# Gated linear attention and two MoE layers: the prefix levels of all four batches taken together, steps laid out by place in their group of four

## The chip, the core and the metric

The kernel runs on one core of one Trainium2 chip. The metric is the device time of one execution in microseconds. The engines named below are PE (matrix products), DVE (vector), ACT (scalar functions and copies), POOL (a second, general engine) and SP (here only an issuer of DMAs).

## What is computed

Four batches of eight heads, 768 steps, 48 dimensions. Attention keeps a complex state of 48 x 48 per head, of which only the real part is fed and read:

```python
mag = sqrt(a_re**2 + a_im**2)
scale = minimum(mag, 0.999) / (mag + 1e-06)
a_re_n, a_im_n = a_re * scale, a_im * scale
for t in range(768):
    S_re, S_im = ar * S_re - ai * S_im + outer(k[t], v[t]), ar * S_im + ai * S_re
    y[t] = q[t] @ S_re
x = tokens(y)                                # 3072 x 384
h = x @ w1_in                                # 384 -> 2048
x = (maximum(h, 0) + alpha * minimum(h, 0)) @ w1_out
h = x @ w2_in
out = where(h >= 1, h, where(h <= -1, 0, (h + 1)**2 / 4)) @ w2_out
```

The weights come as float64 words.

## The kernel before

**Attention.** The steps are cut into six chunks of 128. A *pair* is two batches of one chunk; there are twelve, first batches 0 and 1 for all chunks, then batches 2 and 3. A *slab* is one batch of a pair; `qkh0_1` is that of slab 1 of pair 0. On chip a pair's decays lie in tile `C`, 128 partitions x (re, im) x 6 rows x 129 columns, where column 0 is the carry. For each pair:
- `front` (L155 to L171) normalises the decays; ACT and DVE alternate.
- `scans` (L179 to L185) runs one bounded scan over 768 elements (L182) with the bound `cap`, whose first column takes the carry `mie` of the pair before.
- `levels` takes prefix products of the complex decays with `cmul` (L140 to L147): `ta` within groups of 4 neighbouring steps, `tb` over 4 groups, `tc` and `td` over those, `te` back over the groups. A `cmul` is two multiplications, or four if the shape has more dimensions (L144), into a scratch tile, then one subtraction and one addition back into `C`. With steps in their natural order the operands of `ta` are 16 bytes apart. At its end POOL (L214 to L220) makes the next pair's carry.
- `half`, once for each slab: a last `cmul` (`tf`), two products `qkh` (L231), and 12 DMAs (L235, L238) that restack `qkh` into tile `st`.
- `slab_matmul`: scores `sp` on PE from `st`, `am` = masked scores on DVE (L254), `yp` on PE, then `xbuf` (high part by ACT, L278, low part by DVE, L279), and the update of `state`.

**MoE.** Layer 1 takes blocks of 1, 1, 2, 2, 2, 2 and 2 pairs (256 or 512 columns), layer 2 six blocks of 512. Every product is three matrix products of high and low parts. For each of 16 slices `fc` of the hidden width a block does `h` on PE (9 matmuls, L360), the evacuation, and `acc` on PE (9 matmuls, L392). In layer 1 the evacuation is ACT `u` (L372) and `t` (L373), DVE `t` (L374), ACT `gh` (L380), DVE `gl` (L381).

**Weights.** `load_raw` loads 393 KB of words for each half of a slice; `decode` makes float32 of them in one ACT and four DVE instructions (L306 to L312), 384 elements wide; PE and ACT make the high and low parts (L341 to L346). The loads of slices 7 to 15 are put behind the restacking DMAs of slab 0 of pair 0 in SP's queue.

**Order.** A scheduler sets one static order for each engine when the kernel is built; the instructions of an engine then run in that order, each when its semaphores allow. Evacuations have priority. The source interleaves the steps of attention, of the next pair's `front` and `scans`, and of the decoding:

```python
def attention(p):
    if p + 1 < NPAIR:
        load_pair(p + 1)
    yield from levels(p)
    ahead = prepare(p + 1) if p + 1 < NPAIR else iter(())
    yield from interleave(slabs(p), ahead, SIDE)
    yield from ahead
```

## Time and profile before

| | us |
|---|---|
| median of 3 runs | 1110.85 (1109.9 to 1111.08) |
| profiled execution: span | 1106.8 |
| PE busy | 1008.4 (91%) |
| DVE busy | 853.1 (77%) |
| ACT busy | 515.3 (47%) |
| POOL busy | 96.7 (9%) |

The profiled execution is one of its own; its span runs from the first to the last instruction, and the runs' median is 4.05 us above it, which is what lies around a span. Busy shares are means over the whole program: the first half has attention and layer 1, the second hardly more than matrix products.

### The profile page before, as it was taken

The numbers are of one execution on the slowest core, as the hardware profiler recorded it, in microseconds if no ns is written. First come the engines' busy times: TensorE is split into PE (matmuls) and PEld (weight loads), VectorE is DVE, ScalarE is ACT, GpSimd is POOL, SyncE is SP. The second block draws the span as 40 slices with busy tenths as digits, with TensorE's granted clock in tenths as the row PEclk, the third lists the DMA queues.
The fourth block names the chain that finished last, engine by engine and source line by source line (L and its number), as shares of the span: only waits on it lengthen the run. The fifth ranks groups of instructions, "written<-read, shape, count | busy, mean of one in ns | idle before, by whom it ended". The sixth has DMA issues, their size and how long they took to land.

```text
span 1106.8 us, 16614 instructions
## 1 busy us (share of the span) xinstructions
PE 1008.4 (91%) x6113; PEld 820.4 (74%) x6113; DVE 853.1 (77%) x1858; ACT 515.3 (47%) x920; POOL 96.7 (9%) x116
## 2 busy tenths in 40 slices
...
GB/s 305 80 291 21 113 24 84 97 105 46 102 118 60 114 118 35 147 59 76 122 71 69 51 158 191 144 1 58 1 1 57 1 58 1 1 29 1 29 1 31
DMA packets 59929, 84.93 MB, mean 77 GB/s; under 512 B 7488, under 2 KB 35904, under 8 KB 59840
## 3 DMA queue, kind: packets, MB, share of 16 engines
...
q14 instruction: 39, 0.32, 0.1%
...
## 4 chain that ended last, share of the span: by engine, by line
PE 50%; DVE 31%; DMA 7%; issue 3%; POOL 3%; ACT 2%; SPq 2%; DVEq 0%; ACTq 0%; POOLq 0%
PE acc L392 24%; PE h L360 23%; DVE qkh L231 3%; DVE gl L381 2%; DMA C<-in_ri 2%; DVE C L146 2%; DMA rawhi<-in_w 2%; DVE C L147 2%; DVE t L374 2%; DVE tf L144 2%; DVE ab L182 2%; POOL cw L214 1%; DVE am L254 1%; DMA st<-qkh 1%; DVE C L171 1%
## 5 line engine op out<-in xcount | busy, mean ns | idle before, releaser
L360 PE MATMUL h<-xbuf,whi 128*128 128x512 f32 (+1 forms) x1212 | 374.9, 385 | 4.6 <-ACT wlo L346 3.2
L360 PEld LDWEIGHTS h<-xbuf,whi 128*128 128x128 f32 x1212 | 223.3, 191 | 52.9 <-ACT wlo L346 4.4
L392 PE MATMUL acc<-gl,whi 128*128 128x512 f32 (+1 forms) x606 | 230.1, 383 | 3.7 <-DVE gl L381 3.4
L380 ACT ACTIVATE gh<-t 128x512 fp32r<-128x512 f32 (+1 forms) x208 | 124.4, 598 | 232.3 <-DVE t L374 114.7
L360 PE MATMUL h<-xbuf,wlo 128*128 128x512 f32 (+1 forms) x606 | 231.4, 382 | 0.0
L392 PE MATMUL acc<-gh,wlo 128*128 128x512 f32 (+1 forms) x606 | 228.1, 381 | 0.0
L392 PE MATMUL acc<-gh,whi 128*128 128x512 f32 (+1 forms) x606 | 206.4, 384 | 3.9 <-ACT gh L380 3.3
L381 DVE TENSOR_TENSOR gl<-t,gh 128x512 fp32r<-128x512 f32 (+1 forms) x208 | 134.7, 649 | 67.1 <-ACT gh L380 65.8
L378 DVE TENSOR_TENSOR m<-h,t 128x512 f32<-128x512 f32 x96 | 66.3, 692 | 111.8 <-ACT t L376 111.8
L392 PEld LDWEIGHTS acc<-gl,whi 128*128 128x128 f32 x606 | 114.7, 189 | 29.7 <-DVE gl L381 7.2
L360 PEld LDWEIGHTS h<-xbuf,wlo 128*128 128x128 f32 x606 | 115.7, 191 | 22.3 <-issue 0.2
L392 PEld LDWEIGHTS acc<-gh,wlo 128*128 128x128 f32 x606 | 114.6, 189 | 22.5 <-issue 0.4
L392 PEld LDWEIGHTS acc<-gh,whi 128*128 128x128 f32 x606 | 110.6, 189 | 27.5 <-ACT gh L380 5.2
L376 ACT ACTIVATE t<-h 128x512 f32<-128x512 f32 x96 | 57.5, 599 | 124.5 <-PE h L360 113.6
L372 ACT ACTIVATE u<-h,sg 128x512 f32<-128x512 f32 (+1 forms) x112 | 69.2, 618 | 54.8 <-PE h L360 54.6
L374 DVE TENSOR_TENSOR t<-u,t 128x512 f32<-128x512 f32 (+1 forms) x112 | 68.7, 613 | 27.9 <-ACT t L373 27.9
L252 PE MATMUL sp<-st 96*128 96x128 f32 x384 | 64.2, 300 | 21.4 <-DMA st<-qkh 19.0
L252 PEld LDWEIGHTS sp<-st 96*128 96x128 f32 x384 | 59.7, 212 | 32.1 <-issue 22.6
L344 PE MATMUL wd<-wfirst,ident 128*128 128x384 f32 x64 | 35.4, 649 | 44.3 <-DVE wfirst L312 22.9
L373 ACT ACTIVATE t<-h,sal 128x512 f32<-128x512 f32 (+1 forms) x112 | 69.4, 620 | 6.5 <-DMA x2d<-o 6.5
L379 DVE SCALAR_TENSOR_TENSOR t<-t,m 128x512 f32<-128x512 f32 x96 | 66.1, 691 | 2.6
L214 POOL TENSOR_TENSOR cw<-C 128x12 f32<-128x12 f32 (+1 forms) x13 | 25.6, 1971 | 311.7 <-DVE C L147 311.7
...
## 6 DMA issues: line engine op xcount, KB each, us to landing
...
rawhi<-in_w SPq DMA_DIRECT2D x31, 384.0 KB, 4.5
rawlo<-in_w SPq DMA_DIRECT2D x31, 384.0 KB, 5.0
...
C<-in_ri SPq DMA_DIRECT2D x22, 384.0 KB, 5.8
...
```

The lines of the kernel that those rows point to most:

```text
L214: G.tensor_tensor(w[:, 0:2], co, co, op=ALU.mult)
L252: nc.tensor.matmul(sp[:, h], st[0:96, slot(4 * f + h, 1)], st[0:96, slot(4 * f + h, 0)], start=True, stop=True)
L360: nc.tensor.matmul(hp[:, :n], wt[:, ws], xt[:, kk, :n], start=(k == 0), stop=(k == 8))
L372: A.activation(u[:, :n], hp[:, :n], AF.Copy, scale=sg[:, fc:fc + 1])
L373: A.activation(t[:, :n], hp[:, :n], AF.Copy, scale=sal[:, fc:fc + 1])
L374: V.tensor_tensor(t[:, :n], u[:, :n], t[:, :n], op=ALU.max)
L376: A.activation(t[:, :n], hp[:, :n], AF.Relu, scale=0.5, bias=0.5)
L378: V.tensor_tensor(m[:, :n], hp[:, :n], t[:, :n], op=ALU.max)
L379: V.scalar_tensor_tensor(t[:, :n], t[:, :n], 1.0, m[:, :n], op0=ALU.min, op1=ALU.mult)
L380: A.activation(gh[:, :n], t[:, :n], AF.Copy)
L381: V.tensor_tensor(gl[:, :n], t[:, :n], gh[:, :n].bitcast(F32), op=ALU.subtract)
L392: nc.tensor.matmul(blk["acc"][m][:, :n], wt[:, ws], gt[:, :n], start=(fc == 0 and q == 0), stop=(fc == NFC - 1 and q == 2))
```

## The change

- Pairs go chunk by chunk: pairs 0 and 1 are batches 0 and 1, then 2 and 3, of chunk 0. `levels` takes all twelve rows of a chunk at once (chunk 0 in parts of 3, 3 and 6 rows), so six sets of levels do the work of twelve.
- The 128 steps of a chunk are laid out by their place in the group of four: four runs of 32 columns. `ta` and `tf` then work on runs of 32 neighbours; `tb` steps by 16 bytes. The host lays out inputs and outputs to suit; the mask follows.
- `cmul` writes one product in place and needs half the scratch. Instruction counts of a `cmul` stay.
- The scan runs over the products of groups (33 columns for each row in place of 128), with three small multiplications ahead of it and one (576 elements) behind; `k` is multiplied in `scans`. POOL writes the carry into `cap` itself, and the DVE instruction that did (L179) is gone.
- `C` is twice as large, in two buffers; `q` and `k` have tiles and loads of their own. The second half of chunk 0 is loaded by two DMAs of its own.
- Evacuation of layer 1: one ACT pass and tile `u` go; DVE takes `max(h*sal, t)` straight from PSUM with a scalar for each partition; `gh` and `gl` are multiplied by `sg` in place of the weights, whose own ACT pass (L340 before) goes.
- `decode` is 768 wide: one set of instructions for each slice in place of two.
- The scratch for dynamic DMAs is set to 512.

```diff
     def cmul(name, b, a, dims):
-        sh = [128, 2, *dims]
+        t = t[:, :, 0:w].rearrange(f"p n ({dn}) -> p n {dn}", **{f"d{i}": d for i, d in enumerate(dims)})
         if sum(d > 1 for d in dims) < 3:
-            V.tensor_tensor(t1, a(0).to_broadcast(sh), b, op=ALU.mult)
-            V.tensor_tensor(t2, a(1).to_broadcast(sh), b, op=ALU.mult)
+            sh = [128, 2, *dims]
+            V.tensor_tensor(t, a(1).to_broadcast(sh), b, op=ALU.mult)
+            V.tensor_tensor(b, a(0).to_broadcast(sh), b, op=ALU.mult)
         else:
-            for k in range(4):
-                V.tensor_tensor((t1, t2)[k // 2][:, k % 2], a(k // 2).to_broadcast([128, 1, *dims])[:, 0], b[:, k % 2], op=ALU.mult)
-        yield
-        V.tensor_tensor(b[:, 0], t1[:, 0], t2[:, 1], op=ALU.subtract)
-        V.tensor_tensor(b[:, 1], t1[:, 1], t2[:, 0], op=ALU.add)
-        yield
...
+    def scans(c, js):
+        nj = js.stop - js.start
+        h, o = divmod(js.start, NJ)
+        m = tmps.pop((c, js.start))[:, 2, 0:nj].rearrange("p j (a g) -> p j a g", a=GI)
+        V.tensor_tensor(m[:, :, 2], m[:, :, 2], m[:, :, 3], op=ALU.mult)
+        V.tensor_tensor(m[:, :, 1], m[:, :, 1], m[:, :, 2], op=ALU.mult)
+        f = fac[:, o:o + nj]
+        V.tensor_tensor(f[:, :, 1:], m[:, :, 0], m[:, :, 1], op=ALU.mult)
+        yield
+        s = p1.tile([128, NJ, NG + 1], F32, tag="S", name=f"S{c}_{js.start}")[:, 0:nj]
+        flat = [x.rearrange("p j g -> p (j g)") for x in (s, f, cap[:, js])]
         V.tensor_tensor_scan(flat[0], flat[1], flat[2], 1.0, op0=ALU.mult, op1=ALU.min)
         yield
-        G.tensor_copy(mis[p][:, js], a[:, :, T - 1])
-        A.activation(m2, a, AF.Square)
-        yield
+        V.tensor_tensor(m[:, :, 1:], m[:, :, 1:], s[:, :, 0:NG].unsqueeze(2).to_broadcast([128, nj, GI - 1, NG]), op=ALU.mult)
+        G.tensor_copy(mis[c][:, js], s[:, :, NG])
+        A.activation(m[:, :, 0], s[:, :, 1:], AF.Square)
+        A.activation(m[:, :, 1:], m[:, :, 1:], AF.Square)
+        yield
+        k = ks[2 * c + h][:, o:o + nj]
+        V.tensor_tensor(k, k, m.rearrange("p j a g -> p j (a g)"), op=ALU.mult)
+        yield
...
-        # prefix products: within groups of 4, of 4 groups, of 8 of those with the carry
-        g = C[:, :, :, 1:].rearrange("p n j (g i) -> p n j g i", i=4)
-        for i in range(1, 4):
-            yield from cmul(f"ta{p}_{js.start}__{i}", g[:, :, :, :, i], lambda n: g[:, n:n + 1, :, :, i - 1], (nj, T // 4))
-        e = C[:, :, :, 1:].rearrange("p n j (u w) -> p n j u w", w=16)
-        V.tensor_tensor(q2[:, 1], q2[:, 1], m2, op=ALU.mult)
-        for w in (7, 11, 15):
-            yield from cmul(f"tb{p}_{js.start}__{w}", e[:, :, :, :, w], lambda n: e[:, n:n + 1, :, :, w - 4], (nj, NU))
-        yield from cmul(f"tc{p}_{js.start}_", C[:, :, :, 16], lambda n: C[:, n:n + 1, :, 0], (nj,))
+            A.activation(C[:, :, :, 0], Cs[c - 1][:, :, js, NG], AF.Copy)
+        def place(i):
+            return C[:, :, :, 1 + NG * (GI - 1 - i):1 + NG * (GI - i)]
+        nm = f"{c}_{js.start}"
+        for i in range(1, GI):
+            yield from cmul(f"ta{nm}__{i}", place(i), lambda n: place(i - 1)[:, n:n + 1], (nj, NG))
+        e = place(GI - 1).rearrange("p n j (u v) -> p n j u v", v=4)
+        for w in range(1, 4):
+            yield from cmul(f"tb{nm}__{w}", e[:, :, :, :, w], lambda n: e[:, n:n + 1, :, :, w - 1], (nj, NU))
+        yield from cmul(f"tc{nm}_", C[:, :, :, 4], lambda n: C[:, n:n + 1, :, 0], (nj,))
         for k in (1, 2, 4):
-            z = e[:, :, :, :, 15].rearrange("p n j (y z) -> p n j y z", z=2 * k)
-            yield from cmul(f"td{p}_{js.start}__{k}", z[:, :, :, :, k:], lambda n: z[:, n:n + 1, :, :, k - 1:k], (nj, 4 // k, k))
-        h = C[:, :, :, 0:T].rearrange("p n j (u w) -> p n j u w", w=16)
-        yield from cmul(f"te{p}_{js.start}_", e[:, :, :, :, 3:15:4], lambda n: h[:, n:n + 1, :, :, 0:1], (nj, NU, 3))
-        # |P|^2 MI^2 of the chunk's end: near one, and what is off goes into the carry
-        co = C[:, :, :, T]
-        w = p1.tile([128, 3, nj], F32, tag="cw", name=f"cw{p}_{js.start}")
+            z = e[:, :, :, :, 3].rearrange("p n j (y z) -> p n j y z", z=2 * k)
+            yield from cmul(f"td{nm}__{k}", z[:, :, :, :, k:], lambda n: z[:, n:n + 1, :, :, k - 1:k], (nj, 4 // k, k))
+        h = C[:, :, :, 0:NG].rearrange("p n j (u v) -> p n j u v", v=4)
+        yield from cmul(f"te{nm}_", e[:, :, :, :, 0:3], lambda n: h[:, n:n + 1, :, :, 0:1], (nj, NU, 3))
...
+        w = p1.tile([128, 3, NR], F32, tag="cw", name=f"cw{nm}")[:, :, 0:nj]
         G.tensor_tensor(w[:, 0:2], co, co, op=ALU.mult)
         G.tensor_tensor(w[:, 0], w[:, 0], w[:, 1], op=ALU.add)
         G.tensor_tensor(w[:, 1], mie, mie, op=ALU.mult)
-        G.tensor_tensor(chk[:, p, 0, js], w[:, 0], w[:, 1], op=ALU.mult)
-        G.tensor_copy(chk[:, p, 1, js], mie)
-        G.tensor_scalar(w[:, 2], chk[:, p, 0, js], -0.5, 1.5, op0=ALU.mult, op1=ALU.add)
-        G.tensor_tensor(mie, mie, w[:, 2], op=ALU.mult)
+        G.tensor_tensor(chk[:, c, 0, js], w[:, 0], w[:, 1], op=ALU.mult)
+        G.tensor_copy(chk[:, c, 1, js], mie)
+        if c < NC - 1:
+            G.tensor_scalar(w[:, 2], chk[:, c, 0, js], -0.5, 1.5, op0=ALU.mult, op1=ALU.add)
+            G.tensor_tensor(cap[:, js, 0], mie, w[:, 2], op=ALU.mult)
+    def fixup(c, js):
+        nj = js.stop - js.start
+        C = Cs[c][:, :, js]
+        dst = C[:, :, :, 1 + NG:].rearrange("p n j (a g) -> p n j a g", g=NG)
+        yield from cmul(f"tf{c}_{js.start}", dst, lambda n: C[:, n:n + 1, :, 0:NG].unsqueeze(3), (nj, GI - 1, NG))
...
-            if layer == 1 and s == 1:
-                A.activation(w, w, AF.Copy, scale=sg[:, fc:fc + 1])
...
         if layer == 1:
-            u = p2.tile([128, 512], F32, tag="u", name=f"u{nm}", bufs=UB)
-            A.activation(u[:, :n], hp[:, :n], AF.Copy, scale=sg[:, fc:fc + 1])
-            A.activation(t[:, :n], hp[:, :n], AF.Copy, scale=sal[:, fc:fc + 1])
-            V.tensor_tensor(t[:, :n], u[:, :n], t[:, :n], op=ALU.max)
+            A.activation(t, hp, AF.Copy, scale=sg[:, fc:fc + 1])
+            V.scalar_tensor_tensor(t, hp, sal[:, fc:fc + 1], t, op0=ALU.mult, op1=ALU.max)
+            A.activation(gh, t, AF.Copy, scale=sg[:, fc:fc + 1])
+            V.scalar_tensor_tensor(gl, t, sg[:, fc:fc + 1], gh.bitcast(F32), op0=ALU.mult, op1=ALU.subtract)
...
+    def attention(c):
+        if c + 1 < NC:
+            load_chunk(c + 1)
+            load_k(2 * c + 2)
+        yield from levels(c, ALL)
+        def ahead():
+            yield from prepare(c + 1, HALVES[0])
+            load_k(2 * c + 3)
+            yield from prepare(c + 1, HALVES[1])
+        ahead = ahead() if c + 1 < NC else iter(())
+        yield from interleave(chain(slabs(2 * c), slabs(2 * c + 1)), ahead, SIDE)
         yield from ahead
...
+    load_rows(0, HALVES[1])
+    load_k(1)
+    run(interleave(prepare(0, HALVES[1]), weights, E1))
+    run(interleave(attention_second(), weights, E2))
...
-        while blk["layer"] == 1 and attn < min(NPAIR, blk["p0"] + 4):
+        while blk["layer"] == 1 and attn < min(NC, blk["p0"] // 2 + 2):
```

DVE's order behind the second slab's `qkh` in the kernel before: the products, the next pair's `ta`, its scan and decoding (`wfirst`) follow, and `am0_1_0` stands twenty rows behind them.

```order
L231 TENSOR_TENSOR qkh0_1_524<-C0_109,qk0_117 128x2x384 x2
L140 TENSOR_TENSOR ta1_0__1_852<-C1_613 128x2x192
L141 TENSOR_TENSOR ta1_0__1_852<-C1_613 128x2x192
L311 SCALAR_TENSOR_TENSOR wfirst_95<-rawlo1_3_132,wfirst_95 128x384
L182 SCALAR_TENSOR_TENSOR ab1_616<-m21_617,cap_98 128x768
L307 TENSOR_SCALAR wfirst_95<-wfirst_95 128x384
L146 TENSOR_TENSOR C1_613<-ta1_0__1_852 128x6x32
L147 TENSOR_TENSOR C1_613<-ta1_0__1_852 128x6x32
L312 SCALAR_TENSOR_TENSOR wfirst_95<-rawlo1_3_132,wfirst_95 128x384
L310 TENSOR_SCALAR wfirst_95<-wfirst_95 128x384
L140 TENSOR_TENSOR ta1_0__2_898<-C1_613 128x2x192
L141 TENSOR_TENSOR ta1_0__2_898<-C1_613 128x2x192
```

The same place in the changed kernel: `ab0_6` is the `front` of rows 6 to 11 of chunk 0, whose input is a square that ACT takes of the second half of `C0`.

```order
L263 TENSOR_TENSOR qkh0_1_511<-C0_115,q0_127 128x2x384
L263 TENSOR_TENSOR qkh0_1_511<-C0_115,k0_120 128x2x384
L172 SCALAR_TENSOR_TENSOR ab0_6_594<-ab0_6_594 128x768
L286 TENSOR_TENSOR am0_1_0_533<-sp0_1_0_528,mask_86 128x512
L177 SCALAR_TENSOR_TENSOR ab0_6_594<-ab0_6_594 128x768
L286 TENSOR_TENSOR am0_1_1_540<-sp0_1_1_535,mask_86 128x512
L341 TENSOR_SCALAR wfirst_102<-wfirst_102 128x768
L179 SCALAR_TENSOR_TENSOR ab0_6_594<-ab0_6_594 128x768
```

The work between `qkh0_1` and `am0_1_0` is gone, and one instruction of that `front` stands between them.

SP's queue at the restacking of that slab, before: the last loads of raw weights, `v1_0`, then `st`.

```order
L298 DMA rawhi1_14_411<-in_w1 128x768
L298 DMA rawlo1_14_412<-in_w1 128x768
L298 DMA rawhi1_15_415<-in_w1 128x768
L298 DMA rawlo1_15_416<-in_w1 128x768
L129 DMA v1_0_1193<-in_v 128x544
L235 DMA st_89<-qkh0_1_524 48x768 x4
```

And now: one of the two loads of the second half of `C0`, and `q1`, stand between the raw loads and `st`.

```order
L331 DMA raw1_14_402<-in_w1 128x768 x2
L331 DMA raw1_15_405<-in_w1 128x768 x2
L127 DMA C0_115<-in_ri 128x6x128
L141 DMA v1_0_1091<-in_v 128x544
L137 DMA q1_526<-in_qk 128x768
L267 DMA st_92<-qkh0_1_511 48x768 x4
```

DVE's order around a chunk's end in the changed kernel: POOL's carry starts when the second `td1_0__4` pair has written `C1`, and `S2_0` is the scan that reads it out of `cap`.

```order
L152 TENSOR_TENSOR td1_0__4_1535<-C1_839 128x2x48
L153 TENSOR_TENSOR C1_839<-C1_839 128x24x4
L403 SCALAR_TENSOR_TENSOR t1_1_3_2095<-h1_1_3_2085,sal_112,t1_1_3_2095 128x256
L161 TENSOR_TENSOR C1_839<-C1_839,td1_0__4_1535 128x12x4
L162 TENSOR_TENSOR C1_839<-C1_839,td1_0__4_1535 128x12x4
L405 SCALAR_TENSOR_TENSOR gl1_1_2_2068<-t1_1_2_2066,sg_111,gh1_1_2_2067 128x256
L157 TENSOR_TENSOR te1_0__1540<-C1_839 128x288 x2
L405 SCALAR_TENSOR_TENSOR gl1_1_3_2097<-t1_1_3_2095,sg_111,gh1_1_3_2096 128x256
L159 TENSOR_TENSOR C1_839<-C1_839 128x12x8x3
L403 SCALAR_TENSOR_TENSOR t1_1_4_2121<-h1_1_4_2111,sal_112,t1_1_4_2121 128x256
L159 TENSOR_TENSOR C1_839<-C1_839 128x12x8x3
L202 SCALAR_TENSOR_TENSOR S2_0_1680<-fac_105,cap_107 128x198
```

Six rows stand between the write of `C1` that POOL waits for and the scan.

## Rows read from the trace of the kernel before

**Rows 1.** Whole program: span of the core and mean granted TensorE clock.

```profile
core 0: 1106.8 us, clock 0.977
```

**Rows 2.** Windows: us, busy us (instructions) of each engine, granted clock, DMA share.

```profile
0.00:25.00 25.00, 1.94 (x3) 0.84 (x3) 16.10 (x51) 13.31 (x25) 5.21 (x14) 1.00 0.92 328
50.00:75.00 25.00, 13.54 (x72) 9.49 (x73) 24.79 (x84) 9.46 (x20) 3.23 (x8) 0.88 0.90 321
```

**Rows 3.** Windows from the first `gl` of blocks 2, 3, 4 and 5.

```profile
260.00:352.60 92.60, 86.78 (x634) 71.30 (x635) 88.39 (x201) 44.51 (x73) 11.43 (x16) 0.93 0.32 88
352.60:450.10 97.50, 94.09 (x667) 77.74 (x666) 95.68 (x208) 50.58 (x84) 15.92 (x18) 1.00 0.32 90
450.10:547.40 97.30, 92.94 (x706) 74.80 (x705) 94.11 (x213) 46.75 (x79) 20.58 (x16) 1.00 0.34 97
547.40:628.20 80.80, 79.55 (x613) 65.09 (x612) 48.40 (x105) 37.49 (x63) 2.07 (x6) 1.00 0.23 64
```

**Rows 4.** Timeline of DVE, level `ta` of pair 6: start us, us, instruction.

```profile
311.10 0.85 DVE L140 TENSOR_TENSOR ta__1_3666<-C 128x384 f32<-128x384 f32 x1
311.87 0.85 DVE L141 TENSOR_TENSOR ta__1_3666<-C 128x384 f32<-128x384 f32 x1
313.25 0.50 DVE L146 TENSOR_TENSOR C<-ta__1_3666 128x192 f32<-128x192 f32 x1
313.58 0.50 DVE L147 TENSOR_TENSOR C<-ta__1_3666 128x192 f32<-128x192 f32 x1
```

**Rows 5.** Timeline of DVE, levels `tb` and `te` of pair 5.

```profile
277.15 0.32 DVE L140 TENSOR_TENSOR tb__7_2981<-C 128x96 f32<-128x96 f32 x1
294.07 1.47 DVE L144 TENSOR_TENSOR te__3018<-C 128x144 f32<-128x144 f32 x4
```

**Rows 6.** DVE groups by form: count, busy us, mean ns, idle before.

```profile
L379 DVE SCALAR_TENSOR_TENSOR t<-t,m 128x512 f32<-128x512 f32 x96 | 66.1, 691 | 2.6
L231 DVE TENSOR_TENSOR qkh<-C,qk 128x768 f32<-128x768 f32 x48 | 43.8, 953 | 1.5 <-DMA st<-qkh 1.3
L182 DVE TENSOR_TENSOR_SCAN ab<-m,cap 128x768 f32<-128x768 f32 x11 | 19.3, 1753 | 0.0
L348 DVE TENSOR_TENSOR wlo<-wsecond,whi 128x384 fp32r<-128x384 f32 x30 | 16.4, 553 | 0.0
```

**Rows 7.** Groups of ACT by form.

```profile
L372 ACT ACTIVATE u<-h,sg 128x512 f32<-128x512 f32 x80 | 54.4, 680 | 52.7 <-PE h L360 52.4
L376 ACT ACTIVATE t<-h 128x512 f32<-128x512 f32 x96 | 57.5, 599 | 124.5 <-PE h L360 113.6 <-DMA out<-o 7.5 <-DVE gl L381 2.4
L155 ACT ACTIVATE ab<-C 128x1536 f32<-128x1536 f32 x11 | 16.4, 1488 | 11.7 <-DMA C<-in_ri 11.7
```

**Rows 8.** Timeline of DVE around the second slab of pair 0.

```profile
67.45 1.81 DVE L231 TENSOR_TENSOR qkh<-C,qk 128x768 f32<-128x768 f32 x2
85.93 0.69 DVE L254 TENSOR_TENSOR am<-sp,mask 128x512 f32<-128x512 f32 x1
```

**Rows 9.** Timeline of SP's queue after pair 0's first slab.

```profile
49.11 0.58 SPq L298 DMA_DIRECT2D rawhi<-in_w  x1
63.10 0.33 SPq L298 DMA_DIRECT2D rawlo<-in_w  x1
69.29 2.56 SPq L235 DMA_DIRECT2D st<-qkh  x4
```

**Rows 10.** DMA issues, 38 to 90 us: count, KB, us to landing.

```profile
rawhi<-in_w SPq DMA_DIRECT2D x9, 384.0 KB, 8.0
```

**Rows 11.** Timeline of POOL, the carry of pair 4.

```profile
243.90 11.17 POOL L214 TENSOR_TENSOR cw<-C 128x12 f32<-128x12 f32 x1 [18.66 <-DVE C L147]
256.28 0.20 POOL L220 TENSOR_TENSOR mie<-mie,cw 128x6 f32<-128x6 f32 x1
```

**Rows 12.** Timeline of DVE: the carry reader and block 2 at its start.

```profile
256.52 0.17 DVE L179 TENSOR_TENSOR cap<-m,mie 128x6 f32<-128x6 f32 x1 [1.51 <-POOL mie L220]
260.01 0.69 DVE L381 TENSOR_TENSOR gl<-t,gh 128x512 fp32r<-128x512 f32 x1
```

320 lines of the change are left out of this document (171 added, 149 removed).

## The prediction

> **What bounds the kernel now.** First the span and the clock: 1106.8 us at a mean granted clock of 0.977 [rows 1]. The runs' median, 1110.85 us, lies 4.05 us above that span; the sum below changes the span, and I add it to the median. I call anything within 0.2% (2.2 us) no change, about what a measurement of this kernel can tell.
>
> Then the windows. In the first 25 us DVE is busy 16.1 us, and from then on nearly always (24.8 of 25 from 50 to 75, where PE has only 13.5) [rows 2]. In blocks 2, 3 and 4 of layer 1, together 287.4 us, DVE is busy 88.4 + 95.7 + 94.1 = 278.2 and PE 86.8 + 94.1 + 92.9 = 273.8; from block 5 on PE fills the time (79.6 of 80.8) while DVE has 48.4 [rows 3]. So DVE is the bound until block 5 starts at 547 us, PE close behind it from 260 us, and PE alone after that. Taking work off DVE pays only before 547 us, and there only down to PE's own work.
>
> PE's work in blocks 2 to 4: the first ran at a granted clock of 0.93, which cost 0.07 x 86.8 = 6.1 us, so 273.8 - 6.1 = 267.7 us. That is the floor of this stretch; 287.4 - 267.7 = 19.7 us is the most that can be won there.
>
> **What the levels save.** Durations on DVE overlap, so I price by start-to-start time. Two `ta` multiplications of 384 elements 16 bytes apart start 0.77 us apart though each lasts 0.85; I take 0.085 off every DVE duration [rows 4]. Strided: 384 elements 0.77, and 192 (a subtraction, 0.33 ahead of its addition) 0.33. Contiguous: 384 elements 0.553 - 0.085 = 0.47, 768 elements 0.953 - 0.085 = 0.87 [rows 6], so 0.067 us and 1.04 ns an element.
> - `ta` of a pair: 3 x (2 x 0.77 + 2 x 0.33) = 6.6, of a chunk (two pairs) 13.3. Changed: twelve rows contiguous, 3 x (2 x 0.87 + 2 x 0.47) = 8.0. Saves 5.3.
> - `tb`: 96 elements strided take 0.32 - 0.085 = 0.235 [rows 5], and 192, with one start less, 2 x 0.235 - 0.067 = 0.40. A chunk's twelve multiplications take 2.8, six of the new ones 2.4; the subtractions I take as even. Saves 0.4.
> - `te` of a pair: four multiplications in 1.47 - 0.085 = 1.39 [rows 5], with the shorter subtraction and addition about 1.9; a chunk 3.7. Changed: 288 elements in runs of three, 0.37 each, six of them 2.2. Saves 1.5. `tc` and `td` save 18 starts, 1.2.
> - The scan: 768 elements took 1.753 - 0.085 = 1.67, or 2.1 ns an element [rows 6]; now 198 take 0.48 at most, three products of 192 elements 0.27 each, and one of 576 takes 0.67, so 1.9 against 1.8 with the carry's product. Costs 0.3 a chunk.
>
> Together 5.3 + 0.4 + 1.5 + 1.2 - 0.3 = 8.1; I use 7.9 us of DVE a chunk, the sum over every single instruction, for five chunks. Chunk 0, which stays in parts, saves 4.3. `tf` keeps its six instructions of 288 elements.
>
> **Unknown prices.** `ta` now reads and writes runs of 32: at the contiguous row it saves 5.3 a chunk, at the strided one 0.8. I take the first, since `qkh` over whole rows has it; the second is a rival. In-place writes are bounded by the same two rows. In the evacuation a plain DVE instruction becomes one with a scalar for each partition: nothing more than L379's 691 ns, which has a constant scalar [rows 6], or up to 81 ns more each, as on ACT, where 680 stands against 599 [rows 7]. I take nothing, by the row of the same engine; the upper end is 64 instructions before block 2, 5 us, and 96 in blocks 2 to 4, 7.7 us. Wider decoding saves the start of four instructions, 4 x 0.067 = 0.27 a slice, 4.3 us for layer 1, or nothing if the wide forms take twice the narrow ones. The ACT passes removed, 0.68 us an evacuation [rows 7], are hidden behind DVE, as ACT is half idle. The smaller DMA scratch and the mask have no row that would let them cost time; I take nothing.
>
> **Where the time goes instead: a new stall at 60 us.** The order shows what the summed work hides. Before, some 20 rows of other work stand between `qkh0_1` and `am0_1_0`. DVE's products ended at 69.2, and the second `am0_1` stood at 85.9 with no idle time before it [rows 8]. Changed, one `front` instruction (L172) and the two `am` stand right behind `qkh0_1`. That L172 needs a square by ACT (1.49 us) [rows 7] of the second half of `C0`, and one of that half's two loads stands in SP's queue behind the 18 raw loads.
>
> When does it land? Before, the raws were issued from 49.1 to 63.1 [rows 9], the last landing 8.0 us later, at 71 [rows 10]. Slab 0's `qkh` comes some 3 us earlier by the work saved, so the raws end at about 68, `C0` at 69.5, ACT at 71. DVE's own work would let `qkh0_1` end at 60: what precedes the end of `am0_1_1` adds up to 75 us before and 47 us now, and 44 of the 47 lie before it; add 12 us of start-up waits (8.9 of them in the first 25 us [rows 2]) and 3.3 us of waiting at `am0_0_0`, which has only 3.4 us of other work in front of it, 10.1 before, while restacking and scores need an estimated 6.7 (the first four of twelve issues take 2.6 [rows 9]). So DVE stands from 60 to 71; then `st` of this slab, which shares the queue with `C0` and `q1`, lets `am0_1_0` start at 73 and `am0_1_1` end near 76. There DVE has lost 76 - 47 = 29 us, before 86.5 - 75 = 11.5: 17.5 us more. Of the 28 us saved up to there only 10 show.
>
> **The sum.** Adding start-to-start times along the order, the first `gl` of block 2 has 239 us of DVE work up to it before, and stood at 260.0 [rows 12], so 21 us of waits. Changed it has 233: chunk 0, chunk 1 and the decoding save 16.5, but by then all of chunk 2's levels for four batches are done, where before only one pair of the four was ahead, which takes 10.5 back. 233 + 21 + 17.5 = 271: **+11 us**. The carry's waits of before are among the 21 and kept at their size.
>
> From there DVE has 278.2 - 3 x 7.9 = 254 us for blocks 2 to 4, below PE's 267.7. PE becomes the bound. Of its 13.6 us of idle time (287.4 - 273.8) I keep half, for it also waits on restacking and on transposes: 267.7 + 6.8 = 274.5, **-12.9 us**. From block 5 on PE has 1.2 us to win, **-1**. Sum -2.9: 1110.85 - 2.9 = **1108 us**.
>
> **Rivals.**
> - *The stall is small.* If the second half of `C0` gets through, or the raws drain sooner, the 17.5 us go: 1108 - 17.5 = 1090.5, at half 1099. For it: its load needs 1 us of the queue. Against: the order puts it behind all raws.
> - *The gain in blocks 2 to 4 does not come* because PE's waits have other causes, and DVE in a fixed order makes it wait just as often: 1108 + 12.9 = 1121.
> - *The carry holds DVE*, slower. POOL's chain took 256.48 - 243.90 = 12.6 us once, its first step alone 11.17 where the last took 0.20 [rows 11], and DVE then waited 1.5 [rows 12]. Changed, only six DVE rows (2.5 us) stand between the last write and the scan that reads the carry. At 12.6 us DVE would wait 10 us for each of two carries before block 2 and three behind it. Blocks 2 to 4 have 267.7 - 254 = 13.7 us to spare, so it decides from 4.6 us a chunk on; at 7 us each, +10 before and +7 in them: 1125. A chain that makes DVE wait no longer than the 1.5 us of before stays hidden.
>
>   The Trainium skill ("SBUF — State Buffer", Who interferes with whom) says that a DVE instruction with two SBUF inputs contends with a GpSimd instruction that reads SBUF. The rows on POOL agree, 11.17 us beside 0.20; by that rule a busy DVE always delays the carry, and the time would be the 1125 of this rival.
> - *Runs of 32 cost like strides*: 4.5 us a chunk are not saved, 9 us before block 2, the rest within the margin: 1117.
>
> **Chances.** The forecast 0.42 (1103 to 1113), small stall 0.22, no gain in the blocks 0.16, carry 0.12, strides 0.08. Faster: 0.22 and over half of the forecast, 0.47; no change 0.17; slower 0.36. The range 1091 to 1122 reaches from the whole stall gone to the blocks' gain gone; the ends of small stall and carry outside it hold under 0.2.
>
> **What would show it.** Right: DVE idle for some 11 us before L172 of `ab0_6`, released through ACT by the load of `C0`; `am0_1` near 73 to 76; first `gl` of block 2 near 271; 272 to 277 us from there to block 5; `ta` at 0.95 us for 768 elements. Wrong: DVE idle under 5 us there, a wait for POOL over 4.6 us before each scan, or evacuations on DVE well above 0.69 us.

## The result, and the profile after

The changed kernel takes **1121.05 us** (median of 4 runs, 1118.49 to 1122.06), the kernel before 1110.38 in the same comparison: ratio 1.0092, interval 1.0076 to 1.0107. It is slower by 0.9%, where 1108 us and more likely a gain were forecast. 1121.05 lies just inside the range of 1091 to 1122, but beyond the forecast case's 1103 to 1113.

The profiled run took 1118.49 us. First the span and the clock, which answer to [rows 1]:

```profile
core 0: 1116.5 us, clock 0.961
```

The span is 9.7 us longer than before; the run profiled was the fastest of the four. It took 2.0 us more than its span, so of the 4.05 us between median and span in the kernel before only about half lies around a span, and the rest is the difference from run to run. Windows of the first 275 us (columns as in [rows 2]), and below them the last of these in the kernel before:

```profile
0.00:25.00 25.00, 3.54 (x6) 1.85 (x6) 16.67 (x60) 13.89 (x24) 6.88 (x18) 1.00 0.94 333
50.00:75.00 25.00, 12.60 (x60) 9.15 (x52) 10.86 (x33) 10.00 (x14) 1.37 (x6) 0.76 0.90 317
125.00:150.00 25.00, 11.57 (x43) 8.78 (x41) 24.96 (x58) 12.39 (x19) 3.37 (x7) 0.62 0.00 0
250.00:275.00 25.00, 16.59 (x177) 14.22 (x178) 19.98 (x45) 8.04 (x11) 0.00 (x0) 0.58 0.55 152
```

```profile
250.00:275.00 25.00, 20.02 (x99) 16.78 (x98) 22.34 (x36) 8.62 (x16) 7.32 (x8) 0.86 0.18 48
```

DVE now has two holes, a large one at 50 to 75 us (10.86 busy, 24.79 before) and a small one at 250 to 275 (19.98 busy, 22.34 before). Where the clock reads 0.58 to 0.76, the windows mix stretches at the 1.2 GHz level with stretches at 2.4; PE was busy 12.6, 11.6 and 16.6 us of the 25 in them. From 125 to 150 DVE is full and PE has 11.57 us: chunk 1's levels for all four batches run before its first slab.

The windows from the first `gl` of blocks 2, 3, 4 and 5, which answer to [rows 3]:

```profile
285.80:383.60 97.80, 90.41 (x699) 75.21 (x697) 90.43 (x171) 41.05 (x66) 3.44 (x9) 0.98 0.31 85
383.60:478.40 94.80, 92.48 (x725) 77.92 (x724) 88.75 (x164) 44.84 (x69) 2.43 (x9) 1.00 0.36 100
478.40:562.80 84.40, 84.40 (x695) 71.08 (x697) 74.52 (x148) 30.66 (x50) 1.86 (x6) 1.00 0.28 80
562.80:644.10 81.30, 81.30 (x585) 65.80 (x575) 39.33 (x55) 28.95 (x42) 0.00 (x0) 1.00 0.21 59
```

So the 9.7 us are made up like this:

| stretch | before | after | difference | predicted |
|---|---|---|---|---|
| to block 2's first `gl` | 260.0 | 285.8 | +25.8 | +11 |
| blocks 2 to 4 | 287.4 | 277.0 | -10.4 | -12.9 |
| from block 5 on | 559.4 | 553.7 | -5.7 | -1 |

The first hole, in DVE's timeline and SP's:

```profile
59.05 0.95 DVE L263 TENSOR_TENSOR qkh<-C,k 128x768 f32<-128x768 f32 x1
70.06 0.96 DVE L172 SCALAR_TENSOR_TENSOR ab<-ab 128x768 f32<-128x768 f32 x1 [10.06 <-ACT ab L171]
74.89 0.69 DVE L286 TENSOR_TENSOR am<-sp,mask 128x512 f32<-128x512 f32 x1 [3.87 <-PE sp L284]
76.83 0.69 DVE L286 TENSOR_TENSOR am<-sp,mask 128x512 f32<-128x512 f32 x1 [0.38 <-PE sp L284]
```

```profile
45.46 14.15 SPq L331 DMA_DIRECT2D raw<-in_w  x18
60.32 0.38 SPq L127 DMA_DIRECT2D C<-in_ri  x1
63.26 3.42 SPq L267 DMA_DIRECT2D st<-qkh  x4
```

`qkh0_1` is done at 60.0, L172 starts at 70.06 behind ACT's square of `C0`'s second half, whose load was issued at 60.32 behind 18 raw loads. This is the predicted stall (60, 71, 73 and 76 us).

The second hole was not predicted. SP's queue around 255 us, then PE's first scores behind it, then the `qkh` that this slab restacks:

```profile
252.38 0.33 SPq L137 DMA_DIRECT2D q<-in_qk  x1
253.37 1.86 SPq L127 DMA_DIRECT2D C<-in_ri  x2
255.27 3.76 SPq L132 DMA_DIRECT2D k<-in_qk  x1
259.13 2.48 SPq L267 DMA_DIRECT2D st<-qkh  x4
261.65 6.27 SPq L270 DMA_DIRECT2D st<-qkh  x8
```

```profile
265.52 3.33 PE L284 MATMUL sp<-st 96*128 96x128 f32 x14 [7.06 <-DMA st<-qkh]
```

```profile
252.27 0.95 DVE L263 TENSOR_TENSOR qkh<-C,k 128x768 f32<-128x768 f32 x1
265.06 0.96 DVE L172 SCALAR_TENSOR_TENSOR ab<-ab 128x768 f32<-128x768 f32 x1 [3.22 <-ACT ab L171]
```

The products are done at 253.2, but their restacking is issued from 259.13 on, behind `q`, the two loads of the next `C` (768 KB each) and `k`, whose issue alone holds SP 3.76 us. PE stands 7.06 us for it. The clock adds to the price of the hole: the 14 score matmuls behind it take 3.33 us at the 1.2 GHz level, where at 233.72 us eight of them took 1.05 us at 2.4 GHz.

DVE's groups by form: `m` (L410, with a constant scalar), layer 1's evacuations with a scalar for each partition (L403, L405), and `ta`'s contiguous products (L153), which answer to [rows 6] and [rows 4]:

```profile
L410 DVE SCALAR_TENSOR_TENSOR t<-t,m 128x512 f32<-128x512 f32 x96 | 66.1, 691 | 2.7
L405 DVE SCALAR_TENSOR_TENSOR gl<-t,sg,gh 128x512 fp32r<-128x512 f32 x80 | 59.6, 746 | 16.8 <-ACT gh L404 16.7
L403 DVE SCALAR_TENSOR_TENSOR t<-h,sal,t 128x512 f32<-128x512 f32 x80 | 59.5, 746 | 32.3 <-ACT t L402 32.2
L405 DVE SCALAR_TENSOR_TENSOR gl<-t,sg,gh 128x256 fp32r<-128x256 f32 x32 | 15.3, 477 | 0.0
L153 DVE TENSOR_TENSOR C<-C 128x768 f32<-128x768 f32 x15 | 14.3, 952 | 0.2
```

The carry, POOL's first and last step and the one wait on DVE, which answer to [rows 11, 12]:

```profile
279.99 1.73 POOL L241 TENSOR_TENSOR cw<-C 128x24 f32<-128x24 f32 x1 [42.74 <-DVE C L162]
283.38 0.22 POOL L248 TENSOR_TENSOR cap<-mie,cw 128x12 f32<-128x12 f32 x1
```

```profile
283.63 0.57 DVE L202 TENSOR_TENSOR_SCAN S<-fac,cap 128x198 f32<-128x198 f32 x1 [0.98 <-POOL cap L248]
```

### The profile page after: what moved, and what is told of

Read it like the earlier page. It is cut to its first block, busy times and chain, and to the rows that moved or that the text cites. A ratio compares the mean times of both kernels' runs of the same rounds, so it can differ in the third digit from the quotient of the medians.

```text
span 1116.5 us, 15994 instructions
## 1 busy us (share of the span) xinstructions
PE 1007.7 (90%) x6113; PEld 829.4 (74%) x6113; DVE 818.2 (73%) x1503; ACT 460.6 (41%) x736; POOL 32.9 (3%) x83
## 4 chain that ended last, share of the span: by engine, by line
PE 66%; DVE 18%; DMA 8%; SPq 4%; issue 2%; ACT 1%; POOL 0%; DVEq 0%; ACTq 0%
PE h L389 30%; PE acc L423 30%; DMA raw<-in_w 3%; PE sp L284 3%; SPq L270 2%; DMA C<-in_ri 2%; PE yp L307 2%; DMA st<-qkh 2%; DVE qkh L263 2%; DVE C L153 1%; DVE gl L405 1%; PE dp L316 1%; DVE t L403 1%; DVE C L187 1%; DVE C L161 1%
## 5 line engine op out<-in xcount | busy, mean ns | idle before, releaser
L389 PE MATMUL h<-xbuf,w 128*128 128x512 f32 (+1 forms) x1818 | 435.7, 381 | 8.8 <-DVE t L403 4.4
L423 PE MATMUL acc<-gh,w 128*128 128x512 f32 (+1 forms) x1212 | 391.2, 381 | 8.1 <-ACT gh L404 7.5
L389 PEld LDWEIGHTS h<-xbuf,w 128*128 128x128 f32 x1818 | 326.2, 191 | 75.8 <-DVE t L403 5.5
L423 PEld LDWEIGHTS acc<-gh,w 128*128 128x128 f32 x1212 | 223.5, 189 | 50.7 <-ACT gh L404 8.7
L423 PE MATMUL acc<-gl,w 128*128 128x512 f32 (+1 forms) x606 | 227.9, 380 | 8.7 <-DVE gl L405 8.3
L423 PEld LDWEIGHTS acc<-gl,w 128*128 128x128 f32 x606 | 114.8, 189 | 33.0 <-DVE gl L405 10.3
L402 ACT ACTIVATE t<-h,sg 128x512 f32<-128x512 f32 (+1 forms) x112 | 69.8, 624 | 107.9 <-PE h L389 99.7
L404 ACT ACTIVATE gh<-t,sg 128x512 fp32r<-128x512 f32 (+1 forms) x112 | 73.9, 660 | 85.2 <-DVE t L403 79.4
L403 DVE SCALAR_TENSOR_TENSOR t<-h,sal,t 128x512 f32<-128x512 f32 (+1 forms) x112 | 74.6, 669 | 32.8 <-ACT t L402 32.6
L405 DVE SCALAR_TENSOR_TENSOR gl<-t,sg,gh 128x512 fp32r<-128x512 f32 (+1 forms) x112 | 74.9, 669 | 16.8 <-ACT gh L404 16.7
L410 DVE SCALAR_TENSOR_TENSOR t<-t,m 128x512 f32<-128x512 f32 x96 | 66.1, 691 | 2.7
## 6 DMA issues: line engine op xcount, KB each, us to landing
v<-in_v SPq DMA_DIRECT2D x24, 272.0 KB, 2.8
```

Of the source, the lines that this page charges most:

```text
L389: nc.tensor.matmul(hp[:, :n], wt[:, ws], xt[:, kk, :n], start=(k == 0), stop=(k == 8))
L402: A.activation(t, hp, AF.Copy, scale=sg[:, fc:fc + 1])
L403: V.scalar_tensor_tensor(t, hp, sal[:, fc:fc + 1], t, op0=ALU.mult, op1=ALU.max)
L404: A.activation(gh, t, AF.Copy, scale=sg[:, fc:fc + 1])
L405: V.scalar_tensor_tensor(gl, t, sg[:, fc:fc + 1], gh.bitcast(F32), op0=ALU.mult, op1=ALU.subtract)
L410: V.scalar_tensor_tensor(t, t, 1.0, m, op0=ALU.min, op1=ALU.mult)
```

## The experiments

Ratios are to the kernel before, run beside each variant on the same chip. A variant's difference from the changed kernel compares the two ratios.

Every edit lets the scheduler set a new order, so most variants differ from their twin in more than the edited lines. Of the 1047 instructions that DVE runs up to block 5 in the changed kernel, 35% still have the same kind of instruction in their place in experiment 1, 42% in experiment 2 and 43% in experiment 4; in experiment 12 all have, and so do those of the kernel before in experiment 11. What a trace shows at the edited place is therefore firmer than a difference of a few microseconds in the time.

**1. Fewer raw loads ahead of `C0`'s second half** (of the changed kernel).

```
-R1 = 16
+R1 = 12
```

> Changed kernel with the raw loads of slices 12 to 15 moved behind the second slab's restacking. Theory A (DVE's wait from 60 to 75 us comes from the second half of C0 and the restacking standing behind 18 raw loads): that wait falls from 14 us to under 5, am0_1 ends near 67, the first gl of block 2 comes 8 to 10 us earlier, near 277, and the kernel is 8 to 10 us faster than the changed one, about the time of the kernel before. Rival B (the time lost early is found again anyway, because something else, such as PE's own work or the later raw loads, holds the start of block 2): the wait goes but the kernel stays within 3 us of the changed one.

1111.75 us (10 runs), ratio 1.0017 [1.0003, 1.0032]. The stall shrinks:

```profile
63.03 0.96 DVE L172 SCALAR_TENSOR_TENSOR ab<-ab 128x768 f32<-128x768 f32 x1 [2.96 <-ACT ab L171]
67.20 0.69 DVE L286 TENSOR_TENSOR am<-sp,mask 128x512 f32<-128x512 f32 x1 [3.21 <-PE sp L284]
72.46 0.68 DVE L286 TENSOR_TENSOR am<-sp,mask 128x512 f32<-128x512 f32 x1
```

DVE's wait falls from 14.3 to 6.2 us, not quite to the 5 of theory A. The stall is caused by the queue, and is worth about 8 us. Block 2 came only 3 us earlier (282.7, not 277); block 5, at 552.5, 10.3. In the new order DVE has done 5.8 us more work by block 2's first `gl` (251.3 us busy against 245.5), which is gone from the blocks behind it.

**2. The next chunk's loads behind the restacking** (of the changed kernel).

```
-            load_chunk(c + 1)
-            load_k(2 * c + 2)
+            load_chunk(c + 1, pin=stacked[2 * c - 1, 1])
+            load_k(2 * c + 2, stacked[2 * c - 1, 1])
...
         dma = nc.sync.dma_start(qs[p], qk[c, :, 0, h * NJ:h * NJ + NJ])
+        if p:
+            behind_of(dma, stacked[p - 1, 1])
```

`behind_of` makes SP issue a DMA later than another one; `pin` passes it the last restacking issue of the pair before.

> Changed kernel with the loads of C, k and q of the next chunk put behind the restacking of the slab that frees their tiles in SP's queue. Theory A2 (of the 26 us by which block 2 starts late some 6 to 8 come from a restacking of slab 1 of pair 3 that waits behind q, C3 and k: PE idle 7.1 us before its scores): that idle time falls to under 3 us, block 2's first gl comes 4 to 7 us earlier, the kernel gains 4 to 7 us. Rival B: the loads then come too late for the next front, whose first DVE instruction waits for ACT's square as long as the scores did, and the gain is under 2 us.

**1102.31 us** (4 runs), ratio 0.9920 [0.9899, 0.9942]: 19 us off the changed kernel, where 4 to 7 were expected. SP's queue at the same place, the products that are restacked, and PE's wait for them:

```profile
249.06 2.48 SPq L273 DMA_DIRECT2D st<-qkh  x4
251.59 5.18 SPq L276 DMA_DIRECT2D st<-qkh  x8
256.81 0.58 SPq L141 DMA_DIRECT2D q<-in_qk  x1
257.50 1.21 SPq L127 DMA_DIRECT2D C<-in_ri  x2
```

```profile
246.42 0.95 DVE L269 TENSOR_TENSOR qkh<-C,k 128x768 f32<-128x768 f32 x1
256.84 0.46 PE L290 MATMUL sp<-st 96*128 96x128 f32 x2 [1.19 <-DMA st<-qkh]
```

The restacking is issued 1.7 us after its products instead of 5.9, and PE's longest wait for it falls from 7.1 to 1.2 us. Block 2 starts at 279.9, 5.9 us earlier, as expected. The rest of the gain lies in the blocks behind it, which go at PE's own pace:

```profile
279.90:374.80 94.90, 92.30 (x723) 77.82 (x722) 90.41 (x169) 41.90 (x66) 7.26 (x9) 1.00 0.32 89
374.80:461.40 86.60, 86.60 (x690) 72.94 (x689) 83.79 (x156) 40.86 (x64) 4.58 (x9) 1.00 0.35 96
461.40:547.20 85.80, 85.80 (x685) 72.29 (x683) 77.22 (x152) 34.39 (x54) 3.98 (x7) 1.00 0.27 78
```

267.3 us, 9.7 less than in the changed kernel. PE's largest wait in that stretch, in the changed kernel and here (us in all, how often, longest in us):

```profile
PE dp L316 <- ACT kt L295: 4.7, 2, 2.4
PE dp L322 <- ACT kt L301: 1.1, 1, 1.1
```

None of PE's waits that shrink there names the restacking, so the path by which the edit (or the new order) saves these 9.7 us is not shown. The early stall is still there (24.6 us of DVE idle by 80 us, 25.3 in the changed kernel).

**3. Both.**

> Both orders of SP's queue together. If the two stalls are separate, the gains add: 12 to 16 us below the changed kernel, 2 to 6 us below the kernel before. If both only uncover the same next wait, the sum is under 10 us.

1103.9 us, 0.9935 [0.9914, 0.9956]. Block 2 starts at 272.0, 7.9 us earlier than in experiment 2, but blocks 2 to 4 take 275.6, and block 5 starts at 547.6 as there. The gains do not add: the time stays within noise of experiment 2's.

**4. `gl` without a scalar for each partition** (of the changed kernel; the sign goes back into the weights).

```
-            A.activation(gh, t, AF.Copy, scale=sg[:, fc:fc + 1])
-            V.scalar_tensor_tensor(gl, t, sg[:, fc:fc + 1], gh.bitcast(F32), op0=ALU.mult, op1=ALU.subtract)
+            A.activation(gh, t, AF.Copy)
+            V.tensor_tensor(gl, t, gh.bitcast(F32), op=ALU.subtract)
```

> Changed kernel with the sign put back into the second weights (an ACT pass for each slice), so that gh and gl are a plain copy and a plain subtraction; the first instruction from PSUM keeps its scalar. Theory C (a scalar for each partition costs DVE 62 ns at 512 columns, 56 at 256): gl goes from 747 to about 691 ns, 7 us less DVE work in all, but only some 2 us of them before block 2, where they show; 1 to 3 us faster. Rival D (the scalar is not what makes them longer, the three operands are): gl stays at 747 and the time within 1 us.

1115.72 us (10 runs), 1.0051 [1.0033, 1.0068], about 5 us less, and all of it before block 2 (280.6); blocks 2 to 4 stay at 276.9. The same `gl` falls from 746 and 477 ns to

```profile
L407 DVE TENSOR_TENSOR gl<-t,gh 128x512 fp32r<-128x512 f32 x80 | 54.9, 686 | 13.3 <-ACT gh L406 13.3
L407 DVE TENSOR_TENSOR gl<-t,gh 128x256 fp32r<-128x256 f32 x32 | 13.5, 424 | 0.0
```

**5. The evacuation alone, in the kernel before.** The sign's pass over the weights goes too.

```
-            A.activation(u[:, :n], hp[:, :n], AF.Copy, scale=sg[:, fc:fc + 1])
-            A.activation(t[:, :n], hp[:, :n], AF.Copy, scale=sal[:, fc:fc + 1])
-            V.tensor_tensor(t[:, :n], u[:, :n], t[:, :n], op=ALU.max)
+            A.activation(t[:, :n], hp[:, :n], AF.Copy, scale=sg[:, fc:fc + 1])
+            V.scalar_tensor_tensor(t[:, :n], hp[:, :n], sal[:, fc:fc + 1], t[:, :n], op0=ALU.mult, op1=ALU.max)
+            A.activation(gh[:, :n], t[:, :n], AF.Copy, scale=sg[:, fc:fc + 1])
+            V.scalar_tensor_tensor(gl[:, :n], t[:, :n], sg[:, fc:fc + 1], gh[:, :n].bitcast(F32), op0=ALU.mult, op1=ALU.subtract)
```

> The kernel before, with layer 1's evacuation as in the changed kernel alone (two scalar_tensor_tensor with a scalar for each partition; no pass for u on ACT, no sign folded into the weights). Theory (the pointer scalar costs DVE 60 ns at 512 columns and 53 at 256, two of them an evacuation, in a stretch where DVE is the bound): 3 to 8 us more by block 5's start, and 1114 to 1118 us. Rival (ACT's relief of 0.68 us an evacuation and the shorter chain make up for it): 1108 to 1112 us, block 5 at 547 us as before.

1117.46 us, 1.0060 [1.0038, 1.0083]. Block 2 starts at 255.5, 4.5 us early, but blocks 2 to 4 take 301.7 us instead of 287.4. Block 5 starts 9.8 us later; 96 x 0.06 + 64 x 0.053 would give 9.2. Where DVE is the bound, the scalar's price shows, and the relief of ACT does not pay for it.

**6. The smaller DMA scratch alone, in the kernel before.**

```
-    nc = bacc.Bacc("TRN2", target_bir_lowering=False, num_devices=1)
+    nc = bacc.Bacc("TRN2", target_bir_lowering=False, num_devices=1, dynamic_dma_scratch_size=512)
```

> Kernel before with only the scratch for dynamic DMAs set to 512. This and the next run ask why every matmul of 512 columns starts 230.3 ns after the last in the changed kernel and 233.2 ns in the kernel before, which is 10 us over all matmuls. Theory S (tiles lie at other addresses because the scratch is smaller): the spacing falls to 230 and the kernel is 8 to 10 us faster than before. Theory W (the high and low weights now lie in one tile): spacing 233, time within 2 us of before. Theory R (it differs by chip or day): spacing as in the changed kernel's runs, and the time of the kernel before on the same chip is lower too, so the ratio stays 1.00.

1109.51 us, 1.0000 [0.9991, 1.0010]: nothing.

**7. The wide decoding alone, in the kernel before**, with one weight tile instead of two.

```
-            decode(raw[s], w, PIN and layer == 1)
-            ws.append(w)
-            yield
+        decode(raw, w, PIN and layer == 1)
+        yield
```

> Kernel before with only the wide decoding and the one tile for high and low weights. By the prediction's price 4.3 us less DVE work in layer 1, 2 to 5 us faster if all of it shows. Theory W adds 8 to 10 us by the matmul spacing (230), so 10 to 14 us faster. Theory S or R: spacing 233, 2 to 5 us faster.

1112.82 us, 1.0027 [1.0016, 1.0039]. Block 2 starts at 270.5, 10.5 us late; the whole loses 3. The 4.3 us that the prediction takes off DVE's work did not shorten the program.

**8. The loads behind the restacking, in the kernel before.**

```
+                if p > 1:
+                    behind_of(dma, stacked[p - 2, 1])
...
+        if p:
+            behind_of(dma, stacked[p - 1, 1])
```

The first is `C`'s load, the second `qk`'s.

> Kernel before with its loads of C and of q and k put behind the restacking, as in the run on the changed kernel that gained 19 us. If that gain belongs to the large loads of the change (a chunk's C is 1.5 MB in one go, twice that of a pair), before gains at most 4 us, as its PE waits for restacking add up to 8.5 us in blocks 2 to 4. If the order of loads was a fault of both, before gains 8 us or more and the change itself is still a loss of about as much as measured.

1106.59 us, 0.9971 [0.9951, 0.9991]: the corresponding edit is worth 3 us there against 19 in the changed kernel, so most of what the queue's order costs came with the change.

**9. Experiments 2 and 4, and products that are not written in place** (`tb`, `tc`, `td` go to the other half of the scratch tile).

```
-            V.tensor_tensor(b, a(0).to_broadcast(sh), b, op=ALU.mult)
+            V.tensor_tensor(s, a(0).to_broadcast(sh), b, op=ALU.mult)
```

> Changed kernel with the loads behind the restacking, gl without a scalar for each partition, and the smaller levels (tb, tc, td) multiplied into two scratch tiles in place of one product in place. Less DVE work before block 2 by 2 us for gl and about 3 for the levels: 1098 to 1101, below the run with the loads alone (1102.3). If DVE's work no longer holds block 2, nothing more than 1 us.

1104.92 us, 0.9954 [0.9941, 0.9967]: not the 1098 to 1101 expected, and not below experiment 2.

**10. Experiments 2 and 4.**

> The changed kernel with the next chunk's loads behind the restacking, and gl in layer 1 without the pointer scalar (the sign goes back into the weights). If DVE's work before block 5 still counts when the loads are out of the way: 7 us less DVE work up to block 5, of which a third to a half shows, 1099 to 1101 us. If restacking and scores set the pace there and DVE has slack: 1101 to 1104 us, as with the loads alone (1102.3).

1105.79 us, 0.9948 [0.9927, 0.9968]. A miss of the first case: with the loads out of the way, 7 us less work on DVE bring nothing.

**11. Where the weights lie, in the kernel before.** From 800 to 1080 us PE's matmuls of 512 columns start 233.2 ns apart before (mean over the trace) and 230.3 in the changed kernel, without any wait. Adding up the sizes of the tiles and the DMA scratch that lie ahead of it (no trace prints an address), the first weight tile of layer 2 outside the early ones begins at byte 64992 of each partition before, 32 beyond a multiple of 64, and at 52544, a multiple of 64, in the changed kernel.

```
+    pads = [pool.tile([128, 8], F32, name=f"pad{i}") for i, pool in enumerate((wpool, p1))]
+    for t in pads:
+        nc.gpsimd.memset(t, 0.0)
```

> The kernel before, with two unused tiles of 32 bytes a partition set ahead of the weights, so that the float32r weight tiles start 32 bytes later in each partition; nothing that is computed changes. Theory (where the weights lie in SBUF sets the pace of PE's matmuls): the start-to-start time of 512-column matmuls in layer 2 goes from 233.2 ns to the 230.3 ns of the changed kernel, and the time falls by 8 to 10 us, to about 1101 us. Rival (the pace comes from something else in the changed kernel, such as its DVE or ACT traffic): 233.2 ns stays, and so does the time, 1108 to 1112 us.

1104.6 us, 0.9943 [0.9923, 0.9963], 231.4 ns. One window of layer 2, where PE never idles (the count behind PE's busy time is that of its matmuls, those over the window's edges with them), in the kernel before, in this one, and in the changed one:

```profile
830.00:890.00 60.00, 60.00 (x259) 48.31 (x258) 30.05 (x44) 18.71 (x31) 0.00 (x0) 1.00 0.08 27
```

```profile
830.00:890.00 60.00, 60.00 (x261) 48.75 (x260) 29.58 (x43) 19.12 (x32) 0.00 (x0) 1.00 0.06 23
```

```profile
830.00:890.00 60.00, 60.00 (x263) 48.87 (x262) 31.71 (x45) 20.66 (x33) 0.00 (x0) 1.00 0.08 27
```

**12. The same pads in the changed kernel**, which move its weights off.

> The changed kernel with two unused tiles of 32 bytes a partition ahead of the weights, so that its float32r weight tiles lie 32 bytes further in each partition; nothing that is computed changes. Theory (where the weights lie sets PE's pace): 512-column matmuls of layer 2 start 232 to 233.2 ns apart instead of 230.3, and the time rises by 5 to 10 us, 1126 to 1131 us. Rival (the pace hangs on something else, and the gain of moving them in the kernel before came from the other tiles that moved along): 230.3 ns and 1119 to 1123 us.

1122.74 us, 1.0131 [1.0099, 1.0162], 233.2 ns: the pace goes back.

```profile
830.00:890.00 60.00, 60.00 (x259) 48.22 (x258) 30.73 (x44) 20.31 (x33) 0.00 (x0) 1.00 0.08 27
```

From block 5 on it takes 560.0 us instead of 553.7, and the part up to block 5 came out 2 us shorter (560.7), so the time rises by 4, less than the 5 to 10 expected. The two intervals of the ratio overlap; the pace, with DVE's order unchanged, is what shows the effect. In both pad experiments the tiles behind the weights move along, so the weights' part alone is not separated from theirs.

**13. Experiments 8 and 11 together.**

> The kernel before with the loads of the next pair's C and qk put behind the restacking, and the weight tiles 32 bytes further. If the pace hangs on the address, the two add up: 1106.6 - 9 = about 1098 us, below both kernels and below the best so far (1102.3). If not, 1105 to 1108 us.

1100.97 us, 0.9921 [0.9895, 0.9948], below both kernels. The two ratios multiply to 0.9914, so the gains add. This is also as fast as experiment 2 (0.9920): with the order of its loads and the place of its weights changed, the kernel before is level with the changed one.

**14 to 16. The decoding 384 wide again**, in the changed kernel, in experiment 2 and in experiment 3.

```
-        decode(raw, w, PIN and layer == 1)
-        yield
+        for s in range(2):
+            decode(raw[:, s], w[:, s * DM:s * DM + DM], PIN and layer == 1)
+            yield
```

> The changed kernel with layer 1's and 2's words decoded 384 wide again, in the steps of the kernel before. Theory (a step of decoding twice as wide pushes attention back, as it did in the kernel before, where block 2 came 10.5 us later and the whole 3 us): block 2's first gl at 275 to 281 instead of 285.8, and 1113 to 1118 us. Rival (what is left of block 2's delay is the two stalls and the levels, and the narrow forms only add 4 us of DVE): 286 to 290, 1120 to 1126 us.

> The changed kernel with the next chunk's loads behind the restacking and the words decoded 384 wide. If the wide decoding delays attention: 1096 to 1100 us, less than the 1102.3 of the loads alone. If not: 1102 to 1106 us.

> The changed kernel with twelve instead of sixteen early raw loads, the next chunk's loads behind the restacking and the words decoded 384 wide. If the decoding is what is left of block 2's delay: block 2's first gl at 261 to 266 instead of the 272.0 of the same kernel with wide decoding, and 1096 to 1101 us. If the levels are: 271 to 277, 1103 to 1107 us.

1118.67 us (1.0084 [1.0063, 1.0104]), 1115.27 us (1.0044 [1.0025, 1.0063]) and **1098.16 us (0.9886 [0.9865, 0.9906])**. Against their wide twins that is no clear difference, 14 us more, and 5 us less. Block 2 came at 278.9 in the first, as the theory had it, at 284.5 in the second and at 273.7 in the third, no earlier than the 272.0 of experiment 3; the third's time was that of its first case, but its block 2 came where the second case had it, and the second's time was 15 us off. So the width of the decoding has no price of one sign here. What made the second so slow (its blocks 2 to 4 take 274.1) stays open. The third is the fastest kernel of the study, and its blocks 2 to 4 take 267.4 us, like those of experiment 2.

Over all variants of the changed kernel, the six with the loads behind the restacking (2, 3, 9, 10, 15, 16) take 1098 to 1115 us, and the four without (1, 4, 12, 14) 1112 to 1123.

## Why the prediction was wrong

**The step that failed is block 2's start: "233 + 21 + 17.5 = 271".** It came at 285.8, late in both terms. Counting DVE's instructions up to there start to start, and gaps of over 0.15 us as waits, the kernel before has 245.5 us of work and 14.5 of waits, and the changed one 248.2 and 37.6. (The "239" and "21" for before were off by 6.5 each, which cancels in their sum. Where short gaps end and waits begin moves some 2 us between the two.)

- *Waits: 17.5 us more predicted, 23.1 measured.* The early stall came as drawn, almost to the microsecond: by 80 us DVE has been idle 25.3 us against 9.2, 16.1 more. Behind it DVE waits 14.0 us (78 to 286) against 5.9 before (86 to 261), where "21 us of waits" of before were carried over. Missed was the second hole at 255 us: the change puts `q`, two loads of `C` and `k` ahead of one slab's restacking in SP's queue. I had costed that queue only where it held the raws. With those loads behind the restacking 19 us of the median go (the spans of the two profiles differ by 15.3): block 2 comes 6 us earlier, which the hole explains, and blocks 2 to 4 take 9.7 less, which it does not. This mechanism was none of the rivals.
- *Work: 6 us less predicted, 2.7 more measured.* Two parts. "I take nothing" for the scalar was wrong: L403 and L405 take 475 to 477 ns at 256 columns and 746 at 512. Experiment 4, which separates it for L405, gives 53 and 60 ns (start to start about 60 at either width), against an upper end of 81 taken from ACT. Evacuations take 5.1 us more up to there, 3.8 of it by 64 x 0.06. And by then DVE has also done the front and the scans of half a chunk more (48 `front` instructions against 42: 6.2 us, and 3.3 for the scans), where I had counted only the levels that come earlier ("takes 10.5 back"). The levels themselves went as priced: over the program their products, with `tf`, take 42.7 us less, and the scans with what stood around them (L177 to L182) 1.8 less, 44.5 against 5 x 7.9 + 4.3 = 43.8. The decoding saves 4.1 up to block 2, against 4.3.

The sum also took the wrong path. It adds up DVE alone, as if DVE were the bound up to block 2. In the chain of work that ended last, from 80 us to block 2's first `gl`, DVE has 117 us before and 107 now, but PE goes from 8 to 39 us, SP's issuing from 1 to 21 and the landing of DMAs from 17 to 23; POOL, in the carry, goes from 16 to 3. From 209 to 251 us the chain runs through restacking, scores and PE's other matmuls with hardly an instruction of DVE's. Four slabs follow one another there, and the twelve restacking issues of each hold SP's queue for 8.4 to 8.8 us.

**Blocks 2 to 4: -12.9 predicted, -10.4 measured.** Right in kind: PE is the bound, busy 267.3 us of 277.0, against the floor of 267.7; its idle time is 9.7 us, not the 6.8 that I kept. DVE needed 253.7, by my sum 254. Evacuations take some 14 us more on DVE up to block 5, start to start. In blocks 2 to 4 PE's bound can hide that: taking the scalar from `gl` leaves the stretch at 276.9 in the changed kernel (experiment 4, whose 5 us lie ahead of block 2), and with the loads out of the way (experiments 2 and 10) it brings nothing at all.

**From block 5 on: -1 predicted, -5.7 measured.** PE had no idle time to win; each of its matmuls of 512 columns starts 2.9 ns earlier (1.2%). Where the tiles lie in SBUF is part of that: moving the weights, and what lies behind them, takes off 1.8 of the 2.9 ns in the kernel before, and takes all 2.9 away in the changed one, where the stretch goes from 553.7 back to 560.0 us. What makes the other 1.1 ns is open. This is luck: nothing in the prediction aims at it, and without it the change would have lost some 6 us more.

**The levels.** `ta`'s products take 952 ns for 768 elements, as `qkh` does over whole rows, so contiguous runs of 32 are priced as such; the rival of runs that cost like strides is refuted.

**The carry.** POOL's chain took 3.6 us where 12.6 were feared, and DVE waited 0.98 us once. The Trainium skill ("SBUF — State Buffer", Who interferes with whom) lets DVE and GpSimd exclude each other at a shared port; the first step's 1.73 us beside 0.20 to 0.64 of the later ones fits that, but DVE was busy over the chain's first 2.6 us and the carry was not held for long. The 11.17 us of [rows 11] were no measure for it; what made that step so long before is not shown.

**The rivals.** Small stall, carry and strides are refuted. "The gain in blocks 2 to 4 does not come" gives 1121, the time that came, but not by its reason: most of that gain did come, and was lost before them. That the measured number lay in the range is luck, owed to a case whose reason did not hold. One of the prediction's own signs of being wrong did come: evacuations at 0.746 us where 0.69 was taken.

**The sum, shown part by part.** Loads ahead of the restacking +19, early stall +8, each alone and not additive (both gone: 17); the scalar +5 (`gl` alone, experiment 4) to +7 (the whole evacuation, experiment 5); the weights' place about -4 to -6. The parts come from different kernels with orders of their own and do not add up to the 10 us measured. Without the loads in the way the same change is 0.8% faster than before, and with the early stall gone and narrow decoding 1.1%. But the kernel before with its loads moved and its weights shifted is 0.8% faster too (experiment 13), so a gain from the levels themselves, beyond the order of loads and the weights' place, is not shown.
